# A mixer of cached attention and gated MLP on one core: other PSUM banks for eight transpositions, a longer fetch of x, another order in one row of products

## The chip, the cores and the metric

The kernel runs on one core of a Trainium2 chip. A core has five engines that run side by side, each in its own order of instructions: TensorE (PE; PEld are its weight loads), VectorE (DVE), ScalarE (ACT), GpSimd (POOL) and SyncE (SP), which here only issues DMAs. They wait for each other through semaphores. TensorE writes its products to PSUM, which has eight banks of 128 x 512 numbers in float32. The metric is the device time of one execution in microseconds (us), the median of three.

## What is computed

```python
xn = layernorm(x)                                  # x: 2048 x 512
# branch A: 32 heads of 128, the last 512 positions of the cache
q = xn @ wq                                        # 2048 x 4096, by head
p = softmax(q @ k^T * 128**-0.5)                   # per head 2048 x 512
s = concat_heads(p @ v) @ wo                       # 2048 x 512
# branch B: a gated MLP that mixes positions
z = gelu(xn @ w_in)                                # 2048 x 1376
z1, z2 = z[:, :688], layernorm(z[:, 688:])
g = silu((z1 * (w_sp @ z2 + b_sp)) @ w_out)        # w_sp: 2048 x 2048
out = x + s * g
```

## The kernel before

Every product is made of three matmuls: each operand is held as a rounded high part and the rest (names with `_h` and `_l`, or `wh` and `wl`), and `mm3` adds high x high, high x rest and rest x high (lines 65 to 67 of the kernel; on TensorE's page the first name is the moving one). ACT makes the high part by a copy, and POOL or DVE the rest by a subtraction (line 59).

The order of all work is written by hand: the program is recorded line by line, and each engine's instructions stand in the order of the code. The main loop (`for t in range(T0, T1)`) runs over 512 steps of attention and some before and behind. The queries are cut into two halves of 1024 rows; a block b is one head and 512 rows, four steps. In each step PE makes a score (`score(t)`, 128 x 512, into a step bank), two or three matmuls of the projection of later queries (`q_products`, line 456), a quarter of a product p v (`pv`) and an output product (`outp`, into a step bank). For a score DVE takes the row maxima (line 483), ACT the exp (line 485), which is the last to read the bank. For an output product DVE adds it to the sums (line 542), the last to read that bank. In a step DVE reads the score first, then the output product, and then turns the 32 x 32 squares of the step's p (`turn`, line 494).

A finished block of p goes to memory and back to be transposed as a whole: SP writes 1 MB (line 498) in the step with t % 4 = 0, waits for it to land and reads it back in six pieces (`turned`, line 506) in the step with t % 4 = 2. Five steps after that ACT copies the first quarter of it (`shares`, line 513) and POOL makes the rest (`pT_l`, line 59), and two steps later p v uses them. All these DMAs, the weights' (lines 111 and 417) and those of x stand in one queue on SP, in order.

PSUM in the attention: `ps_acc` has four banks, for p v and for three sums of the query projection. `ps_step` has four single banks `ps_0` to `ps_3`, taken in strict turn by `step_bank`, by scores, output products, transpositions and a few products at either end. The output of p v is read from its bank by ACT (line 528) and last by DVE (`oT_l`, line 59), at the end of the step with t % 4 = 0.

The query projection uses x in seven blocks of sums and differences (`ORDER`), products that save one in eight. The blocks for the second half are made during the first half, in four pairs of row tiles (`later_x(p)`: load, statistics, normalization, transposition of tile b and of tile a, sums, stores), by a table of steps. A transposition is four matmuls against the identity (`flip`, line 208) into one bank, read by ACT copies (lines 299 to 303) and, at the end of the step, by DVE rests and then by `rest_f32` (line 311, tile b) or `row_sums` (lines 243 to 245, tile a). The finished blocks lie in memory. Shortly before the second half's first projection `fetch_part` brings them back, four parts of 256 KB for each of the seven blocks, each block into the place that the first half's last projection has left.

After the attention comes z2 for the 16 row tiles, in the order `ZO` (tiles 8 to 15, then 0 to 7), and then the mixing: for each of 16 rows, 16 chunks c of z2 times a tile of w_sp (`mix`), gating, and the last projection.

## Time and profile before

| | |
|---|---|
| median of three runs | 1830.67 us (1829.18 to 1830.78) |
| the profiled execution | 1831.72 us |
| its span in the profile | 1829.9 us |
| TensorE busy | 1795.9 us, 98% |
| VectorE, ScalarE, GpSimd busy | 76%, 64%, 68% |
| DMA | 394.07 MB, 215 GB/s over the span |

The profile comes from one execution. A row of the timeline gives the start and the duration in us, the engine, the line of the kernel, the operation, output and input, and in brackets the time that the engine stood idle before it and what ended that. Tiles are shown without their numbers: `ps` is a step bank, `ps_a` one of the other four. A row of the waits gives total, number and longest. Matmuls overlap: a row says 0.39 us, but in a full stretch a 128 x 512 matmul starts every 0.227 us.

### The profile page before, as it was taken

The page shows a single profiled execution, that of the slowest core. Times are in us where ns is not written, and L with a number is a line of the kernel's source. Part 1 is how long each engine was busy: PE and PEld are TensorE (multiplying, and loading weights), DVE is VectorE, ACT ScalarE, POOL GpSimd, SP SyncE. Part 2 cuts the span into 40 slices and gives each one's busy share as a digit, 9 for nine tenths or more (in the row PEclk, how much of TensorE's full clock was granted, in tenths as well). Part 3 has the DMA queues.
Part 4 walks back from the last instruction along what each step waited for, and adds up shares of the span by engine and source line. Part 5 has one row for each costly group of instructions (what it writes and reads, how often), then busy time and mean ns, then how long its engine had stood idle before and what let it go on. Part 6 is the DMA issues. An engine that isn't in the chain of part 4 may idle for free.

```text
span 1829.9 us, 28781 instructions
## 1 busy us (share of the span) xinstructions
PE 1795.9 (98%) x8658; PEld 1539.5 (84%) x8658; DVE 1396.6 (76%) x2369; ACT 1172.6 (64%) x2625; POOL 1237.0 (68%) x1179
## 2 busy tenths in 40 slices
PE   8999999999999999999999999999999999999999
PEld 7778787788787887788888888888888999999998
DVE  5689888888898888788888888888888555333333
ACT  4767777777677776677777777777776444333432
POOL 3788898898888887778888888888888343000000
PEclk9999999999999999999999999999999999999999
DMA  5677887887787889687777777777777625554532
GB/s 183 183 242 224 244 266 220 254 250 231 232 266 221 268 240 287 231 254 229 226 224 232 218 223 224 224 225 223 233 219 245 234 94 160 169 181 141 175 127 92
DMA packets 181804, 394.07 MB, mean 215 GB/s; under 512 B 24368, under 2 KB 54832, under 8 KB 164496
## 3 DMA queue, kind: packets, MB, share of 16 engines
q1 hardware_dynamic: 177040, 386.60, 69.3%
q10 hardware_dynamic: 4608, 5.64, 0.9%
q8 instruction: 68, 1.11, 0.3%
q14 instruction: 88, 0.72, 0.1%
HBM read 225.42 MB, written 166.72 MB: 214 GB/s over the span
## 4 chain that ended last, share of the span: by engine, by line
PE 91%; DMA 4%; DVE 3%; ACT 1%; issue 1%; POOL 1%; SPq 0%; ACTq 0%; DVEq 0%; POOLq 0%
PE ps_a L456 15%; PE ps L65 12%; PE ps L67 12%; PE ps L66 12%; PE ps_a L66 8%; PE ps_a L65 8%; PE ps_a L67 8%; PE ps_g L66 4%; PE ps_g L67 4%; PE ps_g L65 4%; DMA pL<-p_dram 2%; DMA p_dram<-pL 1%; PE ps_f L67 1%; PE ps_f L66 1%; PE ps_f L65 1%
## 5 line engine op out<-in xcount | busy, mean ns | idle before, releaser
L59 POOL TENSOR_TENSOR pT_l<-pL,pT_h 128x512 fp32r<-128x512 f32 x507 | 656.3, 1298 | 202.2 <-ACT pT_h L513 180.3
L485 ACT ACTIVATE prob<-ps,nm 128x512 f32<-128x512 f32 x512 | 353.6, 691 | 356.0 <-DVE nm L483 346.2
L542 DVE SCALAR_TENSOR_TENSOR sacc<-ps,sums,sacc 128x512 f32<-128x512 f32 x496 | 370.4, 747 | 144.3 <-PE ps L67 137.8
L456 PE MATMUL ps_a<-x,x 128*128 128x512 f32 x1302 | 377.4, 391 | 0.0
L494 DVE STREAM_TRANSPOSE pL<-prob 128x512 f32<-128x512 f32 x512 | 359.2, 701 | 9.3 <-ACT prob L485 9.3
L483 DVE TENSOR_REDUCE nm<-ps 128x1 f32<-128x512 f32 x512 | 340.4, 665 | 7.0 <-PE ps L67 6.8
L513 ACT CAST pT_h<-pL 128x512 fp32r<-128x512 f32 x512 | 318.4, 622 | 23.9 <-DMA raw<-wh 7.4
L456 PEld LDWEIGHTS ps_a<-x,x 128*128 128x128 f32 x1302 | 245.7, 189 | 51.6
L59 POOL TENSOR_TENSOR wl<-raw,wh 128x512 fp32r<-128x512 f32 x186 | 241.3, 1297 | 11.1 <-ACT wh L150 11.1
L65 PE MATMUL ps<-wh,qT_h 128*128 128x512 f32 x512 | 201.7, 394 | 10.0 <-ACT prob L485 10.0
L65 PE MATMUL ps<-wh,oT_h 128*128 128x512 f32 x512 | 200.1, 391 | 9.9 <-DVE rawx L245 6.5
L66 PE MATMUL ps_a<-pT_l,wh 128*128 128x512 f32 x512 | 200.6, 392 | 1.3 <-POOL pT_l L59 1.2
L66 PE MATMUL ps<-wl,qT_h 128*128 128x512 f32 x512 | 200.2, 391 | 0.0
L67 PE MATMUL ps<-wh,qT_l 128*128 128x512 f32 x512 | 200.1, 391 | 0.0
L65 PE MATMUL ps_a<-pT_h,wh 128*128 128x512 f32 x512 | 200.0, 391 | 0.0
L67 PE MATMUL ps_a<-pT_h,wl 128*128 128x512 f32 x512 | 199.7, 390 | 0.0
L67 PE MATMUL ps<-wh,oT_l 128*128 128x512 f32 x512 | 199.6, 390 | 0.0
L66 PE MATMUL ps<-wl,oT_h 128*128 128x512 f32 x512 | 199.5, 390 | 0.0
L66 PE MATMUL ps_g<-z_l,x 128*128 128x344 f32 x512 | 161.9, 316 | 1.3 <-POOL z_l L59 1.3
L65 PE MATMUL ps_g<-z_h,x 128*128 128x344 f32 x512 | 161.9, 316 | 0.0
L67 PE MATMUL ps_g<-z_h,x 128*128 128x344 f32 x512 | 161.8, 316 | 0.0
L59 POOL TENSOR_TENSOR x<-wq,x 128x256 fp32r<-128x256 f32 x186 | 138.3, 744 | 1.5 <-ACT x L438 1.5
(203 smaller groups left out, 3176.2 us busy)
## 6 DMA issues: line engine op xcount, KB each, us to landing
p_dram<-pL SPq DMA_DIRECT2D x128, 1024.0 KB, 4.9
pL<-p_dram SPq DMA_DIRECT2D x256, 192.0 KB, 3.7
raw<-wh SPq DMA_DIRECT2D x188, 256.0 KB, 6.2
pL<-p_dram SPq DMA_DIRECT2D x256, 128.0 KB, 3.7
pL<-p_dram SPq DMA_DIRECT2D x256, 64.0 KB, 3.4
wq<-wh SPq DMA_DIRECT2D x62, 256.0 KB, 4.7
x<-w_sp SPq DMA_DIRECT2D x60, 256.0 KB, 5.6
x_dram<-rawx SPq DMA_DIRECT2D x32, 256.0 KB, 5.7
```

Of the source, the lines that this page charges most:

```text
L59: engine.tensor_tensor(lo, whole, hi.bitcast(F32), op=OP.subtract)
L65: nc.tensor.matmul(ps, lh, rh, start=first, stop=False)
L66: nc.tensor.matmul(ps, lh, rl, start=False, stop=False)
L67: nc.tensor.matmul(ps, ll, rh, start=False, stop=last)
L456: nc.tensor.matmul(qps[g, bank], wt["q", g, k][a][:, c * P:(c + 1) * P], X[g * 2 // H][ORDER[k]][:, b, c], start=first, stop=r == 5, skip_ ...
L483: nc.vector.tensor_reduce(nm, ps, axis=AX.X, op=OP.max, negate=True)
L485: nc.scalar.activation(prob[t], ps, AF.Exp, bias=nm, accum_out=sums[b][:, j:j + 1])
L494: nc.vector.transpose(pL[b][:, :, j * P:j * P + P].rearrange("p a (c q) -> p a c q", q=Q), prob.pop(t).rearrange("p (a c q) -> p a c q", a ...
L513: nc.scalar.copy(h, p)
L542: nc.vector.scalar_tensor_tensor(at, ps, rs, at, op0=OP.mult, op1=OP.add)
```

## The change

Four edits. First, the transpositions of the second half's tiles (`flip(t[i], True)`) go to `ps_acc` in place of a step bank. Their steps are no longer 30 + 13n/5 alone: each entry of the table comes at least two steps behind the one ahead of it, and the two transpositions of a pair wait for a step with t % 4 = 2. For the first pair nothing moves (steps 50 and 58 as before); in the others the transpositions come at steps 98 and 106 (before 97 and 105), 146 and 154 (144 and 152), 194 and 202 (191 and 199), and the entries behind them move by 0 to 3 steps. Second, `ps_step` is one name with four banks in place of four names with one each: which of them a tile gets is then chosen by the recording layer, not by turns. Third, the 28 parts of x come at step 228 + (35 + 31k + 8n) // 10 for part n of block k, which is from 231 to 252, about four parts in three steps, in place of two parts in each of most steps from 232 to 246; and the parts of a block come in the order in which the products use them. Fourth, the first row of the mixing takes the chunks c in the order `ZO`.

```diff
-    ps_step = psum.enter_context(tc.tile_pool(name="ps_step", bufs=1, space=PSUM))
-    banks = [0]
-
-    def step_bank(shape):
-        banks[0] += 1
-        return ps_step.tile(shape, F32, name=f"ps_{banks[0] % 4}")
+    ps_step = psum.enter_context(tc.tile_pool(name="ps_step", bufs=4, space=PSUM))
...
-    def flip(t):
-        ps = step_bank([P, NC, P])
+    def flip(t, late=False):
+        ps = ps_acc.tile([P, NC, P], F32, name="ps_a") if late else ps_step.tile([P, NC, P], F32, name="ps_3")
...
-        nc.sync.dma_start(X[w][k][:, n // 2, n % 2].bitcast(F32), xd[w, k][:, n // 2, n % 2])
+        nc.sync.dma_start(X[w][k][:, n % 2, n // 2].bitcast(F32), xd[w, k][:, n % 2, n // 2])
...
         def parts(i, n):
-            ps = flip(t[i]).rearrange("p c q -> p (c q)")
+            ps = flip(t[i], True).rearrange("p c q -> p (c q)")
...
-        ps = step_bank([P, W])
+        ps = ps_step.tile([P, W], F32, name="ps_3")
...
-    for k, d in enumerate((4, 6, 8, 11, 13, 15, 17)):
+    for k in range(7):
         for n in range(4):
-            ends.setdefault(16 * (NG // 2 - 1) - LEAD + d + (0, 0, 1, 1)[n], []).append((fetch_part, 1, ORDER[k], n))
+            ends.setdefault(16 * (NG // 2 - 1) - LEAD + (35 + 31 * k + 8 * n) // 10, []).append((fetch_part, 1, ORDER[k], n))
...
-    n = 0
+    n, t = 0, 28
     for p in range(4):
         seq, store = later_x(p)
-        for f, ks in seq:
-            t = 30 + 13 * n // 5
-            for k in ks:
-                at(t, store, k)
+        for k, (f, ks) in enumerate(seq):
+            t = max(t + 2, 30 + 13 * n // 5)
+            while k in (8, 11) and t % 4 != 2:
+                t += 1
+            for key in ks:
+                at(t, store, key)
...
-            for c in (range(4 * part, 4 + 12 * part) if both else range(NT)):
+            for k in (range(4 * part, 4 + 12 * part) if both else range(NT)):
+                c = k if i else ZO[k]
                 for n in (range(2) if both else (part,)):
-                    mm3(us[i][n][:, :NB], c == 0, c == NT - 1, tuple(t[:, c, :] for t in wsp[i]),
+                    mm3(us[i][n][:, :NB], k == 0, k == NT - 1, tuple(t[:, c, :] for t in wsp[i]),
```

What the change moves in the order of the engines is shown at three places. First TensorE at the second transposition of the first pair (step 58), with the semaphores that a row waits for, before: the last matmul of an output product, the transposition, a score, the query projection, p v and the next output product.

```order
L67 MATMUL ps_2461<-wh_1951,oT_l 128x512
L208 MATMUL ps_2478<-ident,rawx 128x128 [waits Activation_49]
L208 MATMUL ps_2478<-ident,rawx 128x128 x3
L65 MATMUL ps_2487<-wh_2271,qT_h 128x512 [waits DVE_49]
L66 MATMUL ps_2487<-wl_2272,qT_h 128x512
L67 MATMUL ps_2487<-wh_2271,qT_l 128x512
L456 MATMUL ps_a<-x_507,x_751 128x512 x3
L65 MATMUL ps_a<-pT_h,wh_2062 128x512
L66 MATMUL ps_a<-pT_l,wh_2062 128x512 [waits Pool_49]
L67 MATMUL ps_a<-pT_h,wl_2063 128x512
L65 MATMUL ps_2501<-wh_2240,oT_h 128x512 [waits Activation_49]
```

And the same place in the change:

```order
L67 MATMUL ps_2461<-wh_1951,oT_l 128x512
L202 MATMUL ps_a<-ident,rawx 128x128 [waits DVE_49,PE_49]
L202 MATMUL ps_a<-ident,rawx 128x128 x3
L65 MATMUL ps_2487<-wh_2271,qT_h 128x512 [waits Activation_49]
L66 MATMUL ps_2487<-wl_2272,qT_h 128x512
L67 MATMUL ps_2487<-wh_2271,qT_l 128x512
L450 MATMUL ps_a<-x_507,x_751 128x512 x3
L65 MATMUL ps_a<-pT_h,wh_2062 128x512 [waits Activation_49]
L66 MATMUL ps_a<-pT_l,wh_2062 128x512 [waits Pool_49]
L67 MATMUL ps_a<-pT_h,wl_2063 128x512
L65 MATMUL ps_2501<-wh_2240,oT_h 128x512 [waits Activation_49]
```

The rows stand in the same place; the transposition's output is now `ps_a`, and it waits for DVE, which reads p v's banks last. Second, TensorE in step 252, in the middle of the attention, from the score to the next step's score, before:

```order
L65 MATMUL ps_9150<-wh_8878,qT_h 128x512 [waits Activation_49]
L66 MATMUL ps_9150<-wl_8879,qT_h 128x512
L67 MATMUL ps_9150<-wh_8878,qT_l 128x512
L456 MATMUL ps_a<-x_8729,x_751 128x512 [waits DMAHW5_49]
L456 MATMUL ps_a<-x_8729,x_751 128x512 [waits DMAHW1_49]
L65 MATMUL ps_a<-pT_h,wh_8671 128x512
L66 MATMUL ps_a<-pT_l,wh_8671 128x512 [waits Pool_49]
L67 MATMUL ps_a<-pT_h,wl_8672 128x512
L65 MATMUL ps_9164<-wh_8845,oT_h 128x512 [waits DVE_49]
L66 MATMUL ps_9164<-wl_8846,oT_h 128x512
L67 MATMUL ps_9164<-wh_8845,oT_l 128x512
L65 MATMUL ps_9183<-wh_8878,qT_h 128x512 [waits Activation_49]
```

And in the change:

```order
L65 MATMUL ps_9149<-wh_8872,qT_h 128x512 [waits DVE_49]
L66 MATMUL ps_9149<-wl_8873,qT_h 128x512
L67 MATMUL ps_9149<-wh_8872,qT_l 128x512
L450 MATMUL ps_a<-x_8768,x_751 128x512 [waits DMAHW6_49]
L450 MATMUL ps_a<-x_8768,x_751 128x512 [waits DMAHW7_49]
L65 MATMUL ps_a<-pT_h,wh_8668 128x512 [waits Activation_49]
L66 MATMUL ps_a<-pT_l,wh_8668 128x512 [waits Pool_49]
L67 MATMUL ps_a<-pT_h,wl_8669 128x512
L65 MATMUL ps_9163<-wh_8839,oT_h 128x512 [waits Activation_49]
L66 MATMUL ps_9163<-wl_8840,oT_h 128x512
L67 MATMUL ps_9163<-wh_8839,oT_l 128x512
L65 MATMUL ps_9183<-wh_8872,qT_h 128x512 [waits DVE_49]
```

The same products in the same order; but the scores, which waited for ACT (the exp two steps back), wait for DVE, and the output product between them, which waited for DVE, waits for ACT. Of all scores some two thirds wait so in the change. Third SP in steps 242 to 246, where `x` are the fetched parts, `p_dram<-pL` a block's write and `pL<-p_dram` its reads, before:

```order
L273 DMA x_8801<-x_dram_108 128x512 x2
L273 DMA x_8871<-x_dram_105 128x512 x2
L498 DMA p_dram<-pL 128x2048
L273 DMA x_8871<-x_dram_105 128x512 x2
L111 DMA raw<-wh 128x512
L273 DMA x_8945<-x_dram_109 128x512 x2
L506 DMA pL<-p_dram 32x3x512
L506 DMA pL<-p_dram 32x512
L506 DMA pL<-p_dram 32x2x512 x2
L506 DMA pL<-p_dram 32x512
L506 DMA pL<-p_dram 32x3x512
L273 DMA x_8945<-x_dram_109 128x512 x2
```

And in the change, in the same steps:

```order
L267 DMA x_8768<-x_dram_107 128x512 x2
L267 DMA x_8866<-x_dram_108 128x512
L492 DMA p_dram<-pL 128x2048
L267 DMA x_8866<-x_dram_108 128x512
L105 DMA raw<-wh 128x512
L267 DMA x_8866<-x_dram_108 128x512
L500 DMA pL<-p_dram 32x3x512
L500 DMA pL<-p_dram 32x512
L500 DMA pL<-p_dram 32x2x512 x2
L500 DMA pL<-p_dram 32x512
L500 DMA pL<-p_dram 32x3x512
L267 DMA x_8866<-x_dram_108 128x512
```

A fetched part fewer stands between the reads of one block and the write of the next, two fewer behind that write, and one block of x has moved down the queue; the fetch goes on for six steps behind this place.

More of the change, by code (lines that the diff above doesn't have):

```diff
@@ L218, in ln_flip @@
         else:
-            ps = step_bank([P, NC, P])
+            ps = ps_step.tile([P, NC, P], F32, name="ps_3")
         rests, rest_of = [], []
@@ L358, in z1_product @@
     def z1_product(i, n, between=lambda: None):
-        ps = ps_acc.tile([P, 512], F32, name="ps_a") if n else step_bank([P, 512])
+        ps = ps_acc.tile([P, 512], F32, name="ps_a") if n else ps_step.tile([P, 512], F32, name="ps_3")
         zmm(ps[:, :NB], i, n, range(2))
@@ L535, in outp @@
         at = sacc[:, i % T8, :]
-        ps = step_bank([P, D])
+        ps = ps_step.tile([P, D], F32, name="ps_3")
         mm3(ps, True, True, cols(oT[b], j * P, (j + 1) * P), wt[("h", h), 3])
@@ L633, in mixer_kernel @@
     nc.vector.memset(power, -0.5)
-    warm = step_bank([P, NC, P])
+    warm = ps_step.tile([P, NC, P], F32, name="ps_3")
     for k in range(21):
@@ L654, in mixer_kernel @@
     split_piece(w0, 3, nc.vector, True)
-    ps = step_bank([P, 512])
+    ps = ps_step.tile([P, 512], F32, name="ps_3")
     zmm_in(FIRST, ps[:, :NB], 0, 0)
@@ L664, in mixer_kernel @@
     ln_open(3)
-    ps = step_bank([P, 512])
+    ps = ps_step.tile([P, 512], F32, name="ps_3")
     zmm_in(PAIRED, ps[:, :NB], 1, 0)
```

## The prediction

> **What bounds the kernel now.** I read the page's table of engines first, then busy time by stretches, then what TensorE (PE) waited for, then the timeline around each of those waits.

> ```profile
> PE 1795.9 (98%) x8658; PEld 1539.5 (84%) x8658; DVE 1396.6 (76%) x2369; ACT 1172.6 (64%) x2625; POOL 1237.0 (68%) x1179
> ```

> PE is the bound: of 1829.9 us it is idle for 34. No matmul is removed or added, so the change can win only those idle microseconds and the time at a reduced clock behind them, and it can lose by making new ones. The waits of PE by their cause, four groups of twelve:

> ```profile
> PE ps L65 <- ACT prob L485: 10.7, 6, 5.5
> PE ps L65 <- DVE rawx L245: 6.5, 4, 2.2
> PE ps L65 <- DVE rawx L311: 3.4, 4, 1.1
> PE ps_g L66 <- POOL z_l L59: 1.3, 1, 1.3
> ```

> (Total us, times, longest.) L245 and L311 are the last VectorE (DVE) readings of a transposition's PSUM bank: four pairs of rows, two transpositions each, eight waits, 9.9 us. The exp's waits are mostly two places, near 95 and 730 us. The last is in the first mixing row. Stretches (PE, PEld, DVE, ACT, POOL busy with counts, granted clock, DMA share, GB/s):

> ```profile
> 300.00:400.00 100.00, 97.51 (x433) 80.07 (x433) 87.41 (x150) 72.88 (x173) 87.00 (x84) 1.00 0.80 244
> ...
> 97.00:101.00 4.00, 4.00 (x12) 3.15 (x11) 1.67 (x4) 3.10 (x9) 4.00 (x5) 0.59 0.53 159
> 461.00:466.00 5.00, 4.74 (x14) 3.79 (x15) 3.89 (x7) 3.00 (x8) 1.75 (x2) 0.66 0.58 239
> 735.00:743.00 8.00, 6.86 (x18) 5.42 (x19) 3.40 (x7) 5.86 (x15) 7.30 (x7) 0.57 0.68 245
> 680.00:735.00 55.00, 49.21 (x215) 39.78 (x213) 43.75 (x72) 34.49 (x82) 39.02 (x37) 1.00 1.01 289
> 1000.00:1300.00 300.00, 300.00 (x1325) 248.49 (x1324) 264.55 (x442) 219.33 (x512) 262.00 (x243) 1.00 0.75 225
> ```

> In the first stretch PE stood still twice, for 2.5 us in all, and the clock stayed full. In the next three it fell, each right behind an idle of 2.2 us or more; they cost 4 x 0.41 = 1.6, 5 x 0.34 = 1.7 and 8 x 0.43 = 3.4 us. The fifth is the fetch of the second half's x: DMA full at 289 GB/s. The last is the undisturbed attention: PE never idle, DMA at 225 GB/s with a quarter free.

> **1. Transpositions into p v's banks, at steps with t % 4 = 2.** The second transposition of the first pair (p = 0), which stood at such a step already:

> ```profile
> 196.89 0.66 DVE L59 TENSOR_TENSOR oT_l<-ps_a,oT_h 128x512 fp32r<-128x512 f32 x1
> 197.25 0.60 PE L208 MATMUL ps<-ident,rawx 128*128 128x128 f32 x4
> ...
> 200.74 0.74 DVE L542 SCALAR_TENSOR_TENSOR sacc<-ps,sums,sacc 128x512 f32<-128x512 f32 x1
> ...
> 203.74 0.42 DVE L245 TENSOR_TENSOR rawx<-ps,rawx 128x256 f32<-128x256 f32 x1
> ...
> 204.32 0.47 PE L65 MATMUL ps<-wh,oT_h 128*128 128x512 f32 x1 [1.66 <-DVE rawx L245]
> ```

> Its bank is held for 6.9 us, from 197.25 to 204.16, and the strict ring of four gives it to the output product two steps on. In p v's pool it is not in that ring, and the same product then takes a bank that an exp had left earlier. All 9.9 us go. What is late next: the transposition itself waits for the bank that p v had two steps before, free when its rest is read, 196.89 + 0.66 = 197.55, against a PE ready at 197.25. I take 0.2 us each (bounds 0 and the 0.3 of this row), 8 x 0.2 = 1.7 back. DVE, 2 us behind here, delays the release of output banks (200.74 + 0.74 = 201.48 for a score that would start at 203.2): covered by 1.7 us. Behind a late transposition the whole step queues on PE. Its bank's next tenant, a q product or p v, comes two to four steps later, hardly longer than the 6.9 us held: cover is thin, and where it goes I estimate 0.5 us a time. With the 2.2 us idle near 459 us the slow clock at 461 goes too. The steps of later pairs move by 1 to 3, and with them activations, sums on POOL (by up to 2 steps, with no reader waiting) and stores, whose DMAs pass from ahead of a block's p write to behind it on SP, where SP waits for that write anyway: nothing. **-9.9 + 1.7 - 1.7 = -9.9** (bounds: -11.6 with no wait left, 0 if the waits come back in the new pool).

> [...] The trace speaks for the idle: of the stretches above the clock fell right behind the longest ones alone.

> **2. Free choice of the four step banks.** Steady steps, before:

> ```profile
> 725.73 0.74 DVE L542 SCALAR_TENSOR_TENSOR sacc<-ps,sums,sacc 128x512 f32<-128x512 f32 x1
> 725.91 0.69 ACT L485 ACTIVATE prob<-ps,nm 128x512 f32<-128x512 f32 x1 [0.59 <-DVE nm L483]
> 727.96 0.39 PE L65 MATMUL ps<-wh,qT_h 128*128 128x512 f32 x1
> ```

> The score at 727.96 needs the bank that exp leaves at 726.60: 1.4 us to spare, and it is this that fails where ScalarE (ACT) is late. The new order makes scores wait on DVE and output products on ACT (shown above): that score takes the bank left at 725.73 + 0.74 = 726.47, 1.5 us to spare, and the exp's bank goes to the output product of the same step, at about 729.8: 3.2 us. So steady steps gain and lose nothing, and a late ACT costs later. The case near 95 us:

> ```profile
> 95.16 1.26 POOL L59 TENSOR_TENSOR pT_l<-pL,pT_h 128x512 fp32r<-128x512 f32 x1 [2.08 <-ACT pT_h L513]
> ...
> 96.64 0.63 PE L65 MATMUL ps<-wh,qT_h 128*128 128x512 f32 x1 [2.21 <-ACT prob L485]
> ...
> 98.29 1.30 POOL L59 TENSOR_TENSOR pT_l<-pL,pT_h 128x512 fp32r<-128x512 f32 x1
> ```

> Without the exp's wait PE goes on from 94.43 and is at p v's second matmul 1.6 us on, at 96.0; its operand comes from POOL at 96.42: 0.4 us. A step later the operand comes at 99.59 and PE is there at 99.1: 0.5. Two waits of 0.9 together in place of 2.2, too short for the clock: **-2.2 + 0.9 - 1.6 = -2.9** (bounds 0 and -3.8).

> **3. x fetched over 22 steps instead of 15.** How it hurts now (SP in order, all in one stretch):

> ```profile
> 708.93 0.71 DVE L494 STREAM_TRANSPOSE pL<-prob 128x512 f32<-128x512 f32 x1 [0.60 <-ACT prob L485]
> 708.95 0.50 PE L65 MATMUL ps<-wh,qT_h 128*128 128x512 f32 x1 [1.41 <-ACT prob L485]
> ...
> 716.27 0.36 SPq L498 DMA_DIRECT2D p_dram<-pL  x1
> ...
> 724.16 3.31 SPq L506 DMA_DIRECT2D pL<-p_dram  x6
> ...
> 733.97 0.62 ACT L513 CAST pT_h<-pL 128x512 fp32r<-128x512 f32 x1 [6.79 <-DMA raw<-wh]
> ...
> 734.66 1.26 POOL L59 TENSOR_TENSOR pT_l<-pL,pT_h 128x512 fp32r<-128x512 f32 x1 [7.58 <-ACT pT_h L513]
> ...
> 736.14 0.79 PE L65 MATMUL ps<-wh,qT_h 128*128 128x512 f32 x1 [5.52 <-ACT prob L485]
> ...
> 737.81 2.50 POOL L59 TENSOR_TENSOR pT_l<-pL,pT_h 128x512 fp32r<-128x512 f32 x2
> ```

> And the same block's path where nothing disturbs it, with the fetch's DMAs and the p reads' usual landing (issues, KB each, us):

> ```profile
> 877.74 0.34 SPq L498 DMA_DIRECT2D p_dram<-pL  x1
> ...
> 881.66 2.66 SPq L506 DMA_DIRECT2D pL<-p_dram  x6
> ...
> 888.17 0.34 SPq L498 DMA_DIRECT2D p_dram<-pL  x1
> ...
> 893.30 0.62 ACT L513 CAST pT_h<-pL 128x512 fp32r<-128x512 f32 x1
> ```

> ```profile
> pL<-p_dram SPq DMA_DIRECT2D x256, 192.0 KB, 3.7
> ```

> ```profile
> x<-x_dram SPq DMA_DIRECT2D x28, 256.0 KB, 5.8
> ```

> The six reads of a block wait on SP for its write to land, and the next block's write queues behind them and the fetch. Undisturbed, a block takes four steps of 2.6 us (877.74 to 888.17), and ACT copies it 15.6 us after its write's issue; the reads landed about 881.66 + 2.66 + 3.7 = 888.0, so 5.3 us are spare. In the fetch DVE finished the block at 709.64 and ACT copied it at 733.97, 24.3 later: 8.7 late with the spare used up, so DMA was 8.7 + 5.3 = 14.0 behind, 15.4 with the 1.4 us that PE had already stood still at 707. The waits of this stretch are 5.5 + 1.4 = 6.9 us.

> After: 28 x 0.262 = 7.3 MB. Spare capacity is 289 - 225 = 64 GB/s. Over the 15 steps of before (39 us) 7.3 - 2.5 = 4.8 MB do not fit, 16.6 us of backlog by this sum against the 15.4 seen. Over 22 steps (57 us) 7.3 - 3.6 = 3.7 MB, 12.8, scaled by 15.4/16.6: 11.9 us. What PE bears without waiting: the 5.3 spare and, with free banks, the time until p v lacks its operand. In the rows above POOL gives it at 735.92 to a PE that would be there at 730.62 + 1.6 = 732.2, and a step later at 739.06 to a PE there at 738.4: 4.4 of wait for 8.7 late, so 4.3 borne. 11.9 - 5.3 - 4.3 = 2.3 us still waited, in pieces, so without a slow clock. **-6.9 + 2.3 - 3.4 = -8.0**; bounds 0 and 15.4 - 9.6 = 5.8 of wait. The fetch's own readers are covered: the last block is asked for at step 250 and used at 258, 21 us on, less 5.8 for the landing, which is more lateness than p v's path bears.

> [...]

> **4. First mixing row in z's order.** The same 96 matmuls. The wait is for the last chunks of z, which now come last:

> ```profile
> 1525.84 0.32 PE L65 MATMUL ps_g<-z_h,x 128*128 128x344 f32 x1
> ...
> 1531.34 1.65 POOL L59 TENSOR_TENSOR z_l<-z,z_h 128x688 fp32r<-128x688 f32 x1 [1.31 <-ACT z_h L800]
> ```

> Chunk 6 is ready at 1532.99; it moves to the fifteenth place, reached 84 matmuls of 0.153 us after 1525.84, at 1538.7. DVE's last chunk comes about 1 us after it and is covered likewise. **-1.3**, with no new wait.

> Sum: -9.9 - 2.9 - 8.0 - 1.3 = -22.1. The profiled execution took 1831.72 us, 1.05 above the median of 1830.67: 1809.6, and against the median **1809 us**.

> **Rivals.** (a) The fetch fits without backlog: 1809 - 2.3 = 1807. For it: the 289 GB/s were seen with SP partly waiting for landings; against it, the share of 1.01. (b) The backlog stays at 15.4, since share 1.01 is reached again and SP issues reads only when a write has landed: 5.8 us of wait and the slow clock return, +3.5 + 3.4: 1816. (c) The transpositions' gain is eaten in p v's pool, where a bank is free only 0 to 1 us before it is wanted: +8.2: 1817. (d) Slower: the output product's bank, released by DVE, now decides when the next-but-one score starts. 1.5 us of cover stands against it; if DVE, 88% busy, exceeded it in every step, 512 steps x 0.1 us would make 1860; it decides from 22.1 / 512 = 0.04 us a step on. Against it: no steady row is near. (e) Nothing gained: PE runs into POOL and DVE, both at 87-88% (262.00 and 264.55 of 300), wherever a stall went: 1831. Against it: in the row 1000:1300 PE is never idle under that load. [...]

> **Numbers.** Forecast 40% (its own range 1805 to 1813), (a) 20%, (b) 15%, (c) 10%, (d) 6%, (e) 4%, (f) 5%. All but (d) and (e) are faster by over 0.2% (3.7 us, about what this measurement can tell): 0.90; same 0.04, slower 0.06. Range 1803 to 1819: below, (a) with the bound of part 2 (0.9) and no wait at the transpositions (1.7), and 1 us for the spread of runs; above, (b) and (c), and 2 us where two of them meet in part.

> **What would show it.** Right: no wait of L65 on L245 or L311; waits of the transposition (now L202) under 0.4 us; full clock around 460 and 95; the first mixing row without a wait on z_l; the p write at most 8 us behind DVE in the fetch. Wrong: an idle of 5 us near 720, waits of scores on L536 spread over all steps, q products waiting for a transposition's readers.

## The result and the profile after

The changed kernel takes 1814.93 us (median of 6 runs, 1812.59 to 1817.71), the kernel before 1830.72 us beside it (6 runs, 1829.18 to 1833.8): a ratio of 0.9911, with a 95% interval of 0.9898 to 0.9923. It is 15.8 us faster where 21.7 were forecast (1830.67 to 1809). The profiled execution took 1814.89 us, its span is 1813.1 us, 16.8 shorter than before. Of all the executions below one, of the kernel with the fetch and the mixing row alone, took 4623.5 us where its four others took 1822.66 to 1826.64; it is left out of that kernel's ratio, though not of its median.

The engines, from the page after:

```profile
PE 1793.2 (99%) x8658; PEld 1538.0 (85%) x8658; DVE 1395.4 (77%) x2369; ACT 1174.4 (65%) x2625; POOL 1237.8 (68%) x1179
```

PE's idle time fell from 34.0 to 1813.1 - 1793.2 = 19.9 us. The causes of its waits after (total us, times, longest):

```profile
PE ps_a L66 <- POOL pT_l L59: 2.8, 4, 0.8
PE ps L65 <- DVE sacc L536: 2.1, 3, 1.6
PE ps_a L65 <- ACT pT_h L507: 1.4, 1, 1.4
PE ps_a L202 <- DVE oT_l L59: 1.2, 4, 0.3
PE ps_a L450 <- DVE oT_l L59: 1.0, 2, 0.8
```

The transpositions' readers (L239 and L305 now, L245 and L311 before), the exp and the mixing row's z_l are gone from the list. New are the transposition's own wait for p v's bank (L202, 0.3 us each), waits on DVE's output addition (L536), of which 1.6 us are one wait in the drain, and two waits of q products (L450). The stretches that answer to those of before:

```profile
90.00:100.00 10.00, 9.93 (x44) 7.89 (x43) 7.85 (x14) 6.64 (x16) 9.33 (x11) 1.00 0.67 205
440.00:480.00 40.00, 39.71 (x177) 32.46 (x176) 36.05 (x64) 29.92 (x71) 33.63 (x33) 1.00 0.85 242
670.00:735.00 65.00, 62.73 (x276) 51.35 (x275) 54.54 (x91) 44.44 (x105) 49.65 (x46) 1.00 0.93 300
735.00:743.00 8.00, 8.00 (x35) 6.15 (x35) 6.90 (x12) 4.88 (x12) 7.23 (x8) 1.00 0.80 276
```

The clock is full at 95, 461 and 735 us. In the fetch p's latest write leaves 728.92 - 721.30 = 7.6 us behind DVE's last transposition of its block, and DMA is still nearly full (0.93, 300 GB/s):

```profile
720.60 0.70 DVE L488 STREAM_TRANSPOSE pL<-prob 128x512 f32<-128x512 f32 x1
```

```profile
728.92 0.38 SPq L492 DMA_DIRECT2D p_dram<-pL  x1
```

PE's waits there, and the longest ones elsewhere, from the timeline (start, us, then in brackets the idle before it and what ended it):

```profile
142.68 0.50 PE L66 MATMUL ps_a<-pT_l,wh 128*128 128x512 f32 x1 [0.85 <-POOL pT_l L59]
145.84 0.47 PE L450 MATMUL ps_a<-x,x 128*128 128x512 f32 x1 [0.81 <-DVE oT_l L59]
733.14 0.50 PE L65 MATMUL ps_a<-pT_h,wh 128*128 128x512 f32 x1 [1.43 <-ACT pT_h L507]
734.48 0.50 PE L66 MATMUL ps_a<-pT_l,wh 128*128 128x512 f32 x1 [0.84 <-POOL pT_l L59]
1400.72 0.43 PE L65 MATMUL ps<-x,x 128*128 128x344 f32 x1 [1.59 <-DVE sacc L536]
```

One table shows where time goes in all the kernels that were run: how much later (+) or earlier (-) each comes through a stretch than the first profile of the kernel before. The borders are the starts of the scores of steps 0, 24, 40, 240, 264 and 511 and PE's last matmul, all read from the timelines; a row's sum is its whole difference. A row is one execution, and it need not be a typical one: that of the second profile of before (1836.92 us) is the slowest of its kernel's eight, that of the filled start (1816.21 us, median 1812.46) the slowest of its four, that of the free choice alone (1824.75 us, median 1820.91) the second slowest of its six. So the table says where time goes, and the medians and ratios say how much.

| kernel | to step 0 | 0-24 | 24-40 | 40-240 | 240-264 | 264-511 | mixing |
|---|---|---|---|---|---|---|---|
| after | +2.85 | -3.62 | +2.58 | -10.54 | -7.33 | +0.95 | -1.63 |
| after, 2nd profile | +3.49 | -4.08 | +0.21 | -10.41 | -4.93 | +0.59 | -1.64 |
| before, 2nd profile | +2.86 | +0.88 | 0.00 | -1.90 | +2.68 | -0.10 | +0.72 |
| after, old transpositions | +1.40 | -2.09 | +1.50 | -9.17 | -5.86 | +0.88 | -1.63 |
| after, strict turn | +5.06 | -3.15 | +1.77 | -10.01 | -6.11 | -0.12 | -1.64 |
| after, old fetch | +2.53 | -3.50 | +0.22 | -9.90 | -0.19 | +0.62 | -1.63 |
| after, x 8 steps later | +1.43 | -2.48 | 0.00 | -4.36 | -6.13 | +0.46 | -1.64 |
| before, moved transpositions | +2.44 | -2.73 | +0.32 | -10.05 | -1.47 | -0.02 | +0.73 |
| before, free choice | +3.11 | -3.43 | +1.25 | -9.22 | -0.32 | +0.67 | +0.73 |
| before, fetch and mixing row | +3.54 | -3.67 | +1.24 | +0.20 | -4.64 | -0.07 | -1.64 |
| after, filled start, drain moved | +1.25 | -3.42 | +1.67 | -9.70 | -4.32 | -0.98 | +0.07 |
| after, fetch over 27 steps | +1.98 | -3.51 | +0.27 | -9.50 | -1.90 | +0.72 | -1.64 |
| filled start, fetch by ScalarE | +1.14 | -3.22 | +0.81 | -10.34 | +5.28 | -0.97 | +0.07 |

### The profile page after: what moved, and what is told of

Its sections match the earlier page's. It is cut to its first block, busy times and chain, and to the rows that moved or that the text cites. A ratio compares the mean times of both kernels' runs of the same rounds, so it can differ in the third digit from the quotient of the medians.

```text
span 1813.1 us, 28712 instructions
## 1 busy us (share of the span) xinstructions
PE 1793.2 (99%) x8658; PEld 1538.0 (85%) x8658; DVE 1395.4 (77%) x2369; ACT 1174.4 (65%) x2625; POOL 1237.8 (68%) x1179
## 4 chain that ended last, share of the span: by engine, by line
PE 89%; DMA 6%; DVE 1%; ACT 1%; POOL 1%; issue 1%; SPq 1%; ACTq 0%; DVEq 0%; POOLq 0%
PE ps_a L450 14%; PE ps L67 12%; PE ps L65 12%; PE ps L66 12%; PE ps_a L66 7%; PE ps_a L67 7%; PE ps_a L65 7%; PE ps_g L65 4%; PE ps_g L67 4%; PE ps_g L66 4%; DMA p_dram<-pL 2%; DMA pL<-p_dram 1%; PE ps_f L67 1%; PE ps_f L65 1%; PE ps_f L66 1%
## 5 line engine op out<-in xcount | busy, mean ns | idle before, releaser
L59 POOL TENSOR_TENSOR pT_l<-pL,pT_h 128x512 fp32r<-128x512 f32 x507 | 656.5, 1298 | 187.6 <-ACT pT_h L507 155.4
L536 DVE SCALAR_TENSOR_TENSOR sacc<-ps,sums,sacc 128x512 f32<-128x512 f32 x496 | 369.6, 746 | 124.7 <-PE ps L67 118.8
L450 PE MATMUL ps_a<-x,x 128*128 128x512 f32 x1302 | 376.0, 389 | 1.0 <-DVE oT_l L59 1.0
L450 PEld LDWEIGHTS ps_a<-x,x 128*128 128x128 f32 x1302 | 244.4, 188 | 52.5 <-PE ps_a L450 1.8
L59 POOL TENSOR_TENSOR wl<-raw,wh 128x512 fp32r<-128x512 f32 x186 | 241.3, 1297 | 11.1 <-ACT wh L144 11.1
L66 PE MATMUL ps_a<-pT_l,wh 128*128 128x512 f32 x512 | 200.1, 391 | 3.0 <-POOL pT_l L59 2.8
L65 PE MATMUL ps_a<-pT_h,wh 128*128 128x512 f32 x512 | 199.5, 390 | 1.5 <-ACT pT_h L507 1.4
L65 PE MATMUL ps<-wh,qT_h 128*128 128x512 f32 x512 | 200.3, 391 | 0.5 <-DVE sacc L536 0.5
L66 PE MATMUL ps<-wl,qT_h 128*128 128x512 f32 x512 | 199.3, 389 | 0.0
L65 PE MATMUL ps<-wh,oT_h 128*128 128x512 f32 x512 | 199.3, 389 | 0.0
L66 PE MATMUL ps<-wl,oT_h 128*128 128x512 f32 x512 | 199.2, 389 | 0.0
L65 PE MATMUL ps_g<-z_h,x 128*128 128x344 f32 x512 | 161.8, 316 | 0.0
L66 PE MATMUL ps_g<-z_l,x 128*128 128x344 f32 x512 | 161.8, 316 | 0.0
L59 POOL TENSOR_TENSOR x<-wq,x 128x256 fp32r<-128x256 f32 x186 | 138.1, 743 | 1.5 <-ACT x L432 1.5
## 6 DMA issues: line engine op xcount, KB each, us to landing
pL<-p_dram SPq DMA_DIRECT2D x256, 192.0 KB, 3.8
raw<-wh SPq DMA_DIRECT2D x188, 256.0 KB, 6.5
wq<-wh SPq DMA_DIRECT2D x62, 256.0 KB, 4.7
x<-w_sp SPq DMA_DIRECT2D x60, 256.0 KB, 5.7
x_dram<-rawx SPq DMA_DIRECT2D x32, 256.0 KB, 6.1
```

Source lines behind the costliest of these rows:

```text
L59: engine.tensor_tensor(lo, whole, hi.bitcast(F32), op=OP.subtract)
L65: nc.tensor.matmul(ps, lh, rh, start=first, stop=False)
L66: nc.tensor.matmul(ps, lh, rl, start=False, stop=False)
L450: nc.tensor.matmul(qps[g, bank], wt["q", g, k][a][:, c * P:(c + 1) * P], X[g * 2 // H][ORDER[k]][:, b, c], start=first, stop=r == 5, skip_ ...
L536: nc.vector.scalar_tensor_tensor(at, ps, rs, at, op0=OP.mult, op1=OP.add)
```

## The experiments

The question: of the forecast's 22.1 us some 5 did not come. Which term failed? The first trace pointed at places outside the change: the start (+2.85), new waits at 140 to 146 us (+2.58) and the drain (+0.95). The rival was that a term of the sum itself was wrong. Times are medians; the kernel before was run beside every group of kernels, 1833.17 us in the first. A ratio is not the quotient of the two medians, and a gain given in us behind it is worked out from the ratio. Its interval is about 0.0013 to either side, 2.4 us, so differences of 1 or 2 us between two kernels are no more than hints unless the traces show them too.

### Each part undone

**The transpositions put back**, in the kernel after:

```diff
-            ps = flip(t[i], True).rearrange("p c q -> p (c q)")
+            ps = flip(t[i]).rearrange("p c q -> p (c q)")
...
-    n, t = 0, 28
+    n = 0
...
-            t = max(t + 2, 30 + 13 * n // 5)
-            while k in (8, 11) and t % 4 != 2:
-                t += 1
+            t = 30 + 13 * n // 5
```

> The kernel after, with the second half's transpositions put back into the step banks at their old steps; the rest stays. Theory (the terms are separate): the waits of the old place come back, about 10 us, 1825 us, with PE waiting on L245 or L311 of the readers of transpositions (their numbers in this kernel's own lines) and a half-clock stretch near 460 us. Rival (the free choice of step banks alone already removes those waits, because a late bank is passed over): at most 3 us back, 1815 to 1818 us, no half clock there.

1818.77 us, ratio 0.9923 (0.9909 to 0.9936). The rival was right: beside the free choice the move is worth 0.0012 of 1831, 2.2 us (3.1 by the second measurement of the kernel after, below), not 10. One line of its waits says how:

```profile
PE ps L65 <- DVE sacc L536: 4.3, 6, 1.5
```

No wait on a transposition's reader is left although the transpositions stand in the step banks again; 2.2 us more of waits on L536 than in the kernel after are what remains of them, in four waits of 0.4 to 0.9 us, less idle than stood ahead of any fall of the clock in the last section. That the free choice passes over the bank that a transposition holds is how I explain it.

**The strict turn put back**, in the kernel after:

```diff
-    ps_step = psum.enter_context(tc.tile_pool(name="ps_step", bufs=4, space=PSUM))
+    ps_step = psum.enter_context(tc.tile_pool(name="ps_step", bufs=1, space=PSUM))
+    banks = [0]
+
+    def step_bank(shape):
+        banks[0] += 1
+        return ps_step.tile(shape, F32, name=f"ps_{banks[0] % 4}")
```

> The kernel after, with the step banks in strict turn again; transpositions, fetch and mixing row stay changed. Theory (free choice is worth its 2.9 us near 95 us and carries 4.3 us of the fetch's lateness, and the 2.85 us lost at the start and 0.95 us lost in the drain have other causes): 1822 us. Rival 1 (free choice itself costs the 2.85 us of the start and the 0.95 us of the drain): 1818 us, with the start and the drain as in the kernel before. Rival 2 (free choice is worth nothing by itself): 1815 us or less.

1816.34 us, 0.9913 (0.9901 to 0.9925): the free choice adds nothing that can be measured once the transpositions are moved. Rival 2 comes nearest. The drain loses nothing here (-0.12 against +0.95), so that loss belongs to the free choice; the start is even later (+5.06), so that one does not. The waits of the exp are back, 7.1 us against 10.7 before, where the kernel after waits on p v's operands (pT_h, pT_l) instead:

```profile
PE ps L65 <- ACT prob L485: 7.1, 8, 2.6
```

**The fetch over 15 steps**, in the kernel after; the order of a block's parts goes back with it, so the two are not told apart:

```diff
-        nc.sync.dma_start(X[w][k][:, n % 2, n // 2].bitcast(F32), xd[w, k][:, n % 2, n // 2])
+        nc.sync.dma_start(X[w][k][:, n // 2, n % 2].bitcast(F32), xd[w, k][:, n // 2, n % 2])
...
-    for k in range(7):
+    for k, d in enumerate((4, 6, 8, 11, 13, 15, 17)):
         for n in range(4):
-            ends.setdefault(16 * (NG // 2 - 1) - LEAD + (35 + 31 * k + 8 * n) // 10, []).append((fetch_part, 1, ORDER[k], n))
+            ends.setdefault(16 * (NG // 2 - 1) - LEAD + d + (0, 0, 1, 1)[n], []).append((fetch_part, 1, ORDER[k], n))
```

> The kernel after, with x fetched over 15 steps as before. Theory (backlog 15.4 us, of which 9.6 are borne with free banks): 5.8 us of wait and a half-clock stretch of 3.4 us in place of 2.3 us of wait, 1822 us. Rival 1 (the backlog hardly changed by the spread; free banks did it all): 1815 us. Rival 2 (free banks bear nothing; the old 6.9 us and 3.4 us come back whole): 1823 us or more.

1820.56 us, 0.9934 (0.9922 to 0.9946): 0.0023 or 0.0028 above the two measurements of the kernel after, 4 to 5 us. By time it lies between the theory and rival 1. By trace, rival 2's reason is right: with free banks and the old fetch, steps 240 to 264 take what they took before (-0.19), so free banks bear none of the lateness that could be told from the 2.7 us by which two profiles of the kernel before differ there. Its other condition, the whole 3.4 us at half clock, did not come: one stretch of 3.41 us fell, not two. The waits of its timeline, the first and the second group of them, and the clock right behind the first:

```profile
699.60 0.50 PE L65 MATMUL ps_a<-pT_h,wh 128*128 128x512 f32 x1 [1.35 <-ACT pT_h L507]
700.94 0.50 PE L66 MATMUL ps_a<-pT_l,wh 128*128 128x512 f32 x1 [0.84 <-POOL pT_l L59]
...
725.29 0.50 PE L65 MATMUL ps_a<-pT_h,wh 128*128 128x512 f32 x1 [1.55 <-ACT pT_h L507]
726.64 0.50 PE L66 MATMUL ps_a<-pT_l,wh 128*128 128x512 f32 x1 [0.84 <-POOL pT_l L59]
```

```profile
701.52:704.93 3.41, 3.41 (x10) 2.64 (x9) 2.00 (x5) 2.51 (x7) 3.41 (x4) 0.50 0.96 359
```

All seven waits there sum to 6.3 us, against 6.9 before. PE no longer stops at a score whose bank the exp holds; it stops a few matmuls further, at p v, whose operand the same late DMA delivers. The wait has changed its place, not its length.

**The second half's x 8 steps later**, in the kernel after:

```diff
-    n, t = 0, 28
+    n, t = 0, 36
...
-            t = max(t + 2, 30 + 13 * n // 5)
+            t = max(t + 2, 38 + 13 * n // 5)
```

> The kernel after, with all of the second half's steps of x, their loads and transpositions among them, 8 steps later. Theory (the new waits at 140 to 146 us come from DMA: the loads of x at step 30 fall on p writes that are late from the start): the 2.6 us of steps 24 to 40 go, 1812.3 us, and the p writes of blocks 6 and 7 are no more than 3 us late. Rival (the lateness is what the start leaves to a faster PE, and the loads of x only show it): the waits stay or come 8 steps later, 1815 us.

1820.14 us, 0.9931 (0.9918 to 0.9943), 4 to 5 us slower than the kernel after where the theory had it 2.6 faster. The waits of steps 24 to 40 are gone, and the p writes of blocks 6 and 7 leave 2.3 and 1.7 us late, as the theory has it. But the second profile of the kernel after has only +0.21 in this stretch, and 40 to 240 here loses 6 us. New there, with 2.6 of the 6 us:

```profile
PE ps L67 <- DVE qT_l L59: 2.6, 4, 0.6
```

So the delay cures a wait that comes and goes, and costs more than it. Most of the rest of the 6 us is no wait of TensorE, and its cause stays open.

### Each part alone, and the same kernels again

Both theories below come from the first four runs: that the move and the free choice are substitutes, and that the loss at the start is chance. The kernel before took 1832.19 us beside these four.

**The move alone**, in the kernel before:

```diff
-            ps = flip(t[i]).rearrange("p c q -> p (c q)")
+            ps = flip(t[i], True).rearrange("p c q -> p (c q)")
...
+            while k in (8, 11) and t % 4 != 2:
+                t += 1
```

> The kernel before with the transpositions' move alone (into p v's banks, at steps of remainder 2). Theory A, formed from the first four runs (either the move or the free choice takes away the old waits on L245 and L311, so each alone has their whole gain): 9.9 us faster than before, no half clock near 460 us; the stall near 95 us stays where the start leaves room for it, and the fetch loses its 10 us. Theory B (the move needs the free choice): under 5 us faster.

1821.61 us, 0.9944 (0.993 to 0.9959): 10.2 us. **The free choice alone**, in the kernel before:

```diff
-        ps = step_bank([P, W])
+        ps = ps_step.tile([P, W], F32, name="ps_3")
```

(and so for the other users of the step banks, whose pool has four banks under one name as in the kernel after)

> The kernel before with the free choice of step banks alone. Theory A (substitutes): the old waits on L245 and L311 go here too, about 9 us, and 2.6 us near 95 us: 11 to 12 us faster than before, with a wait on DVE's sacc of about 1.5 us at the first product of the drain. Theory B (as predicted, the free choice is worth 2.9 us): 3 us faster.

1820.91 us, 0.9945 (0.9931 to 0.996): 10.1 us. Both together, with the old fetch, gave 0.9934, of which the mixing row's 1.6 us are 0.0009: 10.5 us. Three times the same, to within the intervals: each alone brings all that both bring. The table says where: -10.05 and -9.22 between steps 40 and 240. No wait on a transposition's readers is left in either; what stands in their place, with the move and then with the free choice, whose line holds the drain's 1.3 too:

```profile
PE ps_a L208 <- DVE oT_l L59: 1.2, 4, 0.3
```

```profile
PE ps L65 <- DVE sacc L536: 4.3, 7, 1.3
```

Theory A was right, though its 11 to 12 us for the free choice are 1 to 2 too many, and the terms for the two parts must not be added for this stretch.

**The kernel after again** and **the kernel before again**, unchanged:

> The kernel after, unchanged, for a second profile. Theory (the 2.85 us lost at the start are two windows of half clock, and which windows are cut goes by where the clock's windows of 3.41 us happen to lie against the span's start): other windows of the start are cut than at 9.0 and 19.2 us, and step 0 is later than in the kernel before by 0 to 5 us, 1.5 to 1.7 us for each cut window. Rival (the change moves the start): the same two windows, 2.85 us again.

> The kernel before, unchanged, for a second profile. Theory (cut windows at the start are chance): one to three cut windows before 30 us can stand here too, and the stall near 95 us shrinks by as much as step 0 comes later. Rival (they belong to the changed kernel): no cut window before 90 us, and the stall and its half clock near 95 us as in the first profile.

1814.88 us, 0.9906 (0.9893 to 0.992), and 1831.04 us, 0.9991 (0.9977 to 1.0005). The starts of the kernel after and of the kernel before's second profile, each with the 3.41 us before the first fall of the clock, that fall and the second one (PE, PEld, DVE, ACT, POOL busy, then granted clock):

```profile
5.58:8.99 3.41, 1.86 (x12) 1.10 (x10) 2.90 (x7) 1.20 (x4) 1.74 (x2) 1.00 1.00 385
8.99:12.40 3.41, 3.41 (x12) 3.03 (x12) 1.66 (x5) 0.30 (x1) 0.00 (x0) 0.50 0.99 323
19.23:22.64 3.41, 3.41 (x15) 3.35 (x14) 1.96 (x4) 1.00 (x3) 0.00 (x0) 0.50 0.04 12
```

```profile
5.53:8.94 3.41, 1.87 (x11) 1.10 (x9) 2.87 (x7) 1.11 (x4) 1.74 (x2) 1.00 0.99 380
8.94:12.35 3.41, 3.35 (x12) 3.06 (x12) 1.75 (x5) 0.39 (x2) 0.00 (x0) 0.50 1.01 341
19.18:22.59 3.41, 3.41 (x15) 3.35 (x14) 1.93 (x4) 1.00 (x3) 0.00 (x0) 0.50 0.02 5
```

The kernel before, unchanged, falls at the same two places and comes to step 0 by 2.86 us later than in its first profile. The second profile of the kernel after has its falls there too, at 9.5 and 19.8 us, where I had expected others. So the loss at the start is none of the change; the first profile of before was one without a fall at the start. In other profiles one stretch fell there (the fetch over 27 steps, at 16.9 us), or three (the strict turn, at 8.3, 18.5 and 28.8 us). My expectation for the second half was wrong: the stall near 95 us did not shrink by as much in this run (+0.88), and in the kernel with only the fetch and the mixing row changed, which is the same up to there, it was gone (-3.67). That stall too comes and goes.

**The fetch and the mixing row alone**, in the kernel before:

```diff
-        nc.sync.dma_start(X[w][k][:, n // 2, n % 2].bitcast(F32), xd[w, k][:, n // 2, n % 2])
+        nc.sync.dma_start(X[w][k][:, n % 2, n // 2].bitcast(F32), xd[w, k][:, n % 2, n // 2])
...
-    for k, d in enumerate((4, 6, 8, 11, 13, 15, 17)):
+    for k in range(7):
...
-            ends.setdefault(16 * (NG // 2 - 1) - LEAD + d + (0, 0, 1, 1)[n], []).append((fetch_part, 1, ORDER[k], n))
+            ends.setdefault(16 * (NG // 2 - 1) - LEAD + (35 + 31 * k + 8 * n) // 10, []).append((fetch_part, 1, ORDER[k], n))
...
+                c = k if i else ZO[k]
```

> The kernel before with the longer fetch and the mixing row's order alone; the step banks in strict turn and the transpositions as before. Theory A (the fetch is worth the 8.0 us of the prediction by itself, and the mixing row 1.6): 9.6 us faster than before. Theory B (it is worth the 4 to 5 us by which the earlier runs with and without it differ): 6 us faster. Both expect the old waits on L245 and L311 and the half clock near 460 us to stay.

1826.42 us beside 1832.85, 0.9958 (0.9945 to 0.9971): 7.7 us by the ratio, 6.4 by the medians, between the theories; less the mixing row's 1.6, the fetch is worth 6.1 or 4.8 by itself. What both theories expected to stay, stays:

```profile
PE ps L65 <- ACT prob L485: 7.4, 7, 2.6
PE ps L65 <- DVE rawx L245: 6.8, 4, 2.2
PE ps L65 <- DVE rawx L311: 3.4, 4, 1.1
```

```profile
463.23:466.64 3.41, 3.41 (x10) 2.62 (x9) 3.02 (x5) 2.33 (x6) 1.07 (x1) 0.50 0.58 243
```

### The start, the drain and what is left in the fetch

**Filled idles and the drain's bank**, in the kernel after:

```diff
+    junk = ps_acc.tile([P, NC, P], F32, name="ps_a")
+
+    def keep_busy(n):
+        for k in range(n):
+            nc.tensor.transpose(junk[:, k % NC, :], ident, ident)
+
+    keep_busy(4)
...
+                if h:
+                    keep_busy(2)
...
+            if n and k in (2, 3):
+                keep_busy((6, 2)[k - 2])
...
-        ps = ps_acc.tile([P, 512], F32, name="ps_a") if n else ps_step.tile([P, 512], F32, name="ps_3")
+        ps = ps_acc.tile([P, 512], F32, name="ps_a") if n or i >= T8 else ps_step.tile([P, 512], F32, name="ps_3")
...
+            if t == T0:
+                keep_busy(5)
```

> The kernel after, with 19 extra transpositions of the identity into a bank that nobody reads, put where TensorE stands still before 30 us, and with the drain's z1 products all in p v's banks. No window of half clock should be left before 30 us, and step 0 should come 2 to 3 us earlier than in the two profiles of the kernel after. Theory A (the start's loss is taken back by the stall near 95 us anyway, which the p writes through DRAM set, so it is not what is missing from the forecast): step 24 stands where it stood, and the whole is 0.6 us faster, from the drain's wait on L536 alone. Theory B (the start's loss goes through to the end): 3 to 3.5 us faster than the kernel after.

1812.46 us, 0.9885 (0.9871 to 0.9899), the best of all: 0.0021 and 0.0026 below the two measurements of the kernel after, with intervals that overlap a little. No clock fell at the start (granted clock 1.00 throughout); and one wait is new, at the beginning of the mixing:

```profile
5.00:30.00 25.00, 20.58 (x131) 17.91 (x129) 18.31 (x40) 10.31 (x29) 8.43 (x13) 1.00 0.59 208
```

```profile
1511.04 0.43 PE L65 MATMUL ps_g<-z_h,x 128*128 128x344 f32 x1 [0.55 <-ACT z L791]
```

Step 0 comes 1.6 and 2.2 us earlier than in the two profiles after, step 24 by 1.4 and 1.6. So most of the start's loss goes through to step 24, against theory A; at step 40 the lead over the second profile is 0.1 us. By the ratio the whole is 3.9 or 4.8 us faster, as theory B has it, but the profiled execution, the slowest of its four, is 1.3 us slower than the two of the kernel after and cannot show where. The drain's gain does not last: -0.98 instead of +0.95 up to step 511, and the mixing takes 1.7 us of it back (+0.07 instead of -1.63). Of that, 0.55 is the wait shown. The rest is a slower pace behind it: at full clock the same 120 matmuls take 1537.97 - 1519.03 = 18.94 us, and 1536.79 - 1518.39 = 18.40 in the kernel after, and so for some 30 us. Why, no run here shows.

**The fetch over 27 steps** (226 to 252; the expectation says 28), in the kernel after:

```diff
-            ends.setdefault(16 * (NG // 2 - 1) - LEAD + (35 + 31 * k + 8 * n) // 10, []).append((fetch_part, 1, ORDER[k], n))
+            ends.setdefault(16 * (NG // 2 - 1) - LEAD + (-15 + 39 * k + 10 * n) // 10, []).append((fetch_part, 1, ORDER[k], n))
```

> The kernel after, with the fetch begun 5 steps earlier and spread over 28 steps. Theory A (the wait left in the fetch, 2.3 and 4.1 us in two profiles, is the rest of the DMA backlog): waits near 733 us under 1 us, 2 to 3 us faster than the kernel after. Theory B (the backlog only moves, or the earlier transfers meet others): the same time as the kernel after or slower.

1819.1 us, 0.9924 (0.9911 to 0.9936): 2 to 3 us slower than the kernel after, theory B. The waits now come at both ends:

```profile
700.87 0.50 PE L65 MATMUL ps_a<-pT_h,wh 128*128 128x512 f32 x1 [1.56 <-ACT pT_h L507]
702.22 0.50 PE L66 MATMUL ps_a<-pT_l,wh 128*128 128x512 f32 x1 [0.84 <-POOL pT_l L59]
...
736.53 0.50 PE L65 MATMUL ps_a<-pT_h,wh 128*128 128x512 f32 x1 [1.12 <-ACT pT_h L507]
737.88 0.50 PE L66 MATMUL ps_a<-pT_l,wh 128*128 128x512 f32 x1 [0.85 <-POOL pT_l L59]
```

So the lateness does not go by bytes per step alone, which the prediction's backlog sum took it to do.

**The fetch issued by ScalarE**, in the kernel with filled idles:

```diff
-        nc.sync.dma_start(X[w][k][:, n % 2, n // 2].bitcast(F32), xd[w, k][:, n % 2, n // 2])
+        nc.scalar.dma_start(X[w][k][:, n % 2, n // 2].bitcast(F32), xd[w, k][:, n % 2, n // 2])
```

> The previous kernel with filled idles at the start and the drain in p v's banks, and besides the 28 fetch transfers issued by ScalarE instead of SP; nothing else differs from it. Theory A (what makes p late in the fetch is SP's order: the writes and reads of p stand behind fetch issues that stand behind a landing): p writes at most 3 us late in steps 228 to 262, waits there under 1 us, 2 to 4 us faster than the previous kernel, ratio near 0.987. Theory B (it is the load on the DMA engines: a p write that lands in 4.5 us elsewhere takes 7 us there, whoever issues the fetch): writes still land in 7 us, the waits stay at 3 us, and the time is the same as the previous kernel's, ratio near 0.9885, or slower by what ScalarE spends on issuing.

1823.32 us beside 1830.69, 0.9956 (0.9944 to 0.9968): 13 us slower (0.0071) than the kernel it was made from, and theory A is refuted. SP's queue in the kernel after (p's writes and reads, and the fetch between them), then here:

```profile
703.86 0.38 SPq L492 DMA_DIRECT2D p_dram<-pL  x1
...
710.77 3.21 SPq L500 DMA_DIRECT2D pL<-p_dram  x6
714.02 1.84 SPq L267 DMA_DIRECT2D x<-x_dram  x3
...
717.39 0.57 SPq L492 DMA_DIRECT2D p_dram<-pL  x1
718.22 1.30 SPq L267 DMA_DIRECT2D x<-x_dram  x2
724.74 2.66 SPq L500 DMA_DIRECT2D pL<-p_dram  x6
```

```profile
685.62 0.37 SPq L496 DMA_DIRECT2D p_dram<-pL  x1
...
690.70 7.66 SPq L504 DMA_DIRECT2D pL<-p_dram  x6
...
710.29 0.37 SPq L496 DMA_DIRECT2D p_dram<-pL  x1
...
716.89 7.54 SPq L504 DMA_DIRECT2D pL<-p_dram  x6
```

A block's round on SP, write to write, is 717.39 - 703.86 = 13.5 us against the 10.4 that four steps take, and 6.9 of it is the write's landing. Without the fetch on SP the write still takes 5.1 to 7.3 us to land, as theory B has it, and besides the six reads need 6.0 to 8.8 us to issue in four of the rounds, two of them shown, where the kernel after needs 2.7 to 3.4. Theory B's time, the same or a little slower, is missed too: steps 240 to 264 take 9.6 us more than in the kernel with filled idles, about half in waits and half at half clock. ScalarE's own time is not the cause: it stood idle for 6.4 us before the late copies at 688.35 and 729.48, until a DMA had landed. Behind a landing on SP, the fetch came in when p's traffic left room; issued from elsewhere it comes at its step whatever p needs. That it is this pacing is my reading; the rows show the reads' longer issue and the same landing.

## Why the prediction was right, and where it was not

The direction and the range held, and in the first profile every sign that was to show the steps right: no wait on a transposition's readers, L202 at 0.3 us, full clock near 95 and 460 us, no wait on z_l, the p write 7.6 us behind DVE in the fetch. In the second profile the latest p write is 729.60 - 720.96 = 8.6 us behind, over the 8 of the sign. The time is 5.9 us above the forecast.

**Transpositions: right in size and place, wrong as a sum.** -10.54 and -10.41 us came where -9.9 was forecast (four waits of 0.3 on p v's bank, 1.2 us, for the 1.7 charged; 8 x 0.2 is 1.6). Against the second profile of the kernel before it is 8.6: the 1.7 us at half clock near 461 are missing there, behind the same idle.

```profile
464.67 0.47 PE L65 MATMUL ps<-wh,oT_h 128*128 128x512 f32 x1 [2.16 <-DVE rawx L245]
```

So the waits are a steady cost of the kernel before, and the slow clock behind them is not: of three profiles with this idle two show it. What the step missed is that the second part removes the same waits by itself: a wait on a bank in strict turn goes when its tenant leaves, and also when the turn goes. The forecast lost nothing by it, since it charged the waits once, but it put them to one part of two that are each enough.

**Free choice: -2.9 was mis-sized.** Its evidence was the stall near 95 us. Step 24 was reached, against the first profile of before, at 0, +3.7, -0.1, -0.3 and +1.9 us by the five profiles with strict turn, at -0.3 to -1.5 by the seven with free choice whose start was not filled: a mean of 1.0 against -0.8. That is 1.9 us, of a stall that an unchanged kernel shows or doesn't; the five lie 4 us apart, so it is a rough figure. Against it stands the drain, which the step did not look at: +0.5 to +1.0 in all seven, 0 to -0.1 in the five, from the z1 product that waits on DVE (1.6 us, above) where it waited on the exp before:

```profile
1415.83 0.43 PE L65 MATMUL ps<-x,x 128*128 128x344 f32 x1 [0.64 <-ACT prob L485]
```

Net 1.2, less than the times can tell; with the transpositions moved, the kernels with and without the free choice differ by 0.0002 to 0.0007.

**Fetch: -8.0 was mis-sized, and this is the largest miss.** The seven profiles with 22 steps issued by SP have a mean of -5.6 between steps 240 and 264, the five with the old 15 one of +0.1: 5.8 us; by time it is 4 to 6. The step that failed is that PE bears 4.3 us more of lateness with free banks: with the old fetch, free choice has -0.2 and -0.3 there, strict turn 0, +2.7 and -1.5; with the new, -5.7 and -5.4 on average. The clock was the other half: in place of the 3.4 us of the first profile, the three kernels with the old fetch and one or both of the first two parts lose one stretch of 3.41 us at half clock, 1.7 us. The waits left with the new fetch, 2.3 forecast, are 2.3 and 4.1 us in the two profiles of the kernel after and 2.5 to 5.0 in the five others, in one of them (the filled start, 3.1) with a fall of the clock besides. They lie within the forecast's own bounds (0 to 5.8 of wait). How much of the gain is the spread and how much the order of a block's parts was not tested.

**Mixing row: right in its cause,** -1.63 or -1.64 for the -1.3 forecast, in the eight profiles that have it with the old drain. The first profile of before is here the lucky one too: the three others with the old row take 0.7 us longer in the mixing (+0.72 and +0.73), at the slower pace that is described under the filled start, so against them the row is worth 2.4.

Together 10 + 1.2 + 5.8 + 1.6 = 18.6 us against the 15.8 and 17.3 (1832.19 - 1814.88) of the two measurements. What is left is within what two profiles of one kernel differ by in one stretch (up to 2.9 us in the table), and I do not put it to a cause. The three places outside the change that the first trace pointed to were the drain, which is real, and the start and the waits near 142 us, which come and go.

**The rivals.** (d), the bank that DVE leaves, decided at one place in the drain and in the steady steps twice, for 0.5 us together. (f), that the slow stretches at 97 and 461 are no work of the idles and stay, is refuted: 461 is at full clock in every kernel without the 2.2 us idle before it. Of the three profiles that have the idle, two are at half clock behind it and one, the second of before, is not. (c) did not come: 1.2 us. (a) and (b) lie on either side of what the fetch showed: waits of 2.3 and 4.1 us where (a) had none and (b) 5.8 with a fall of the clock. (e) is refuted by the time.

## What to carry to other kernels

Two edits that each free the same bank are one gain (here 10.2 and 10.1 us alone, 10.5 together): ask of every wait which of them ends it, and try each alone. A wait on a late operand is not won by freeing the consumer's bank; it is found again at the next place where the operand is used (here 6.3 us of waits in place of 6.9), so its lateness must be shortened. One profile's stalls of 2 to 4 us at the start of a run may be chance: take a second profile of the unchanged kernel before a term is built on one.

## What was not expected of the hardware

```profile
733.47 0.50 PE L65 MATMUL ps_a<-pT_h,wh 128*128 128x512 f32 x1 [2.15 <-ACT pT_h L507]
```

```profile
100.32 0.50 PE L65 MATMUL ps<-wh,qT_h 128*128 128x512 f32 x1 [1.95 <-ACT prob L485]
```

In the first 30 us, with matmuls of 128x128 and 128x344, a sum of 1.31 us was followed by a fall in one case (before with the fetch and the mixing row, at 9.3 us) and an idle of 1.71 us was not in another (filled start, up to 7.70 us). Of the 14 falls behind the first 60 us ten lasted 3.41 us and four 6.83; at a granted clock of 0.50 the shorter ones cost 1.7 us of work each where TensorE had work throughout. What sets the 3.413 us, and what else decides, no run here shows.
